# Keys transposed one phase at a time, one filter tile evacuated by VectorE, mixing outputs laid out anew, and new constants in the scheduler, in a gated mixer kernel

## The chip, the cores and the metric

The kernel runs on one core of one Trainium2 chip. The metric is the device time of one execution in microseconds (us), the median of several runs of the same kernel. The profile's span of an execution is 1.7 to 2.1 us shorter than its timed run, because it leaves out the start and the end of the execution.

Five engines matter. TensorE does the matmuls. VectorE does elementwise work and statistics. ScalarE mainly copies matmul results out of PSUM, the memory into which TensorE writes. GpSimd does small elementwise steps. SyncE issues the transfers (DMA). Each engine runs its own list of instructions in order, and engines wait for one another by semaphores. In the profile they are called PE (with PEld for weight loads), DVE, ACT, POOL and SP.

## The reference

The inputs are bfloat16, with S = 2048 positions and D = 640 channels. Two branches are computed from x and mixed by a gate.

```python
g = sigmoid((x * gate_w).sum(-1, keepdims=True))
# branch a: short filter of the keys, times v, long causal convolution by FFT, times q (q is x)
k_shift = sum over t < 4 of k_pad[:, t:t+S, :] * shift_k[:, 3-t]
kv = k_shift * v
y  = irfft(rfft(kv, 2S) * rfft(ssm_k, 2S))[:S] + kv * ssm_D
a  = q * y
# branch b: layernorm, then an MLP over the positions
h = layernorm(x)
u = gelu(einsum("bsd,sf->bdf", h, w1) + b1)
b = transpose(einsum("bdf,fs->bds", u, w2) + b2)
out = g * a + (1 - g) * b
```

## The kernel before

The convolution is a discrete Fourier transform done by matmuls with a table (`FTB` forward, `GTB` inverse). The positions are split into four phases (position modulo 4). TensorE transforms each phase, ScalarE copies the result to a slot of a tile `C`, and VectorE combines the slots with additions and subtractions of 128x2560 or 128x5120 elements. This is called mixing. The filter goes through it first. Then come the two halves of the product k_shift * v. The first is called `vkv` in the traces and the second `kv`. The matmuls that form k_shift have `KT`, the transposed keys, as the stationary operand and `DG`, a table of diagonal matrices, as the moving one. `X` is the layernormed input of the MLP, `ring` holds its weights, and `pp` is any PSUM buffer. In the layernorm, VectorE writes `stats` and `mv` (mean and variance), and GpSimd makes `rstd` (the reciprocal of the standard deviation) from `mv` in two short steps, `vtmp` and `rstd`. `junk` is the product with the gate's weights.

The keys are loaded with a transposing DMA in blocks of channels. The positions of one phase therefore lie four apart in a row, and the stationary operand is read with a stride of four elements:

```python
KT = [alloc(f"KT{i}", [128, ND, 1040], BF16) for i in range(2)]
def kT_load(h, db):
    dma(KT[h][:, db, 16:1040], A_k[0, 1024*h:1024*h+1024, db*128:db*128+128], ..., transpose=True, chain=True)
# in kv(hk): seven matmuls for each block of 128 channels
for q in range(4):
    items.append((..., V(KT[h], base + q, [[4, 128]]), DG[:, db, 0:4 - q, :]..., q == 0, False))
```

The filter is transposed on TensorE, and all 16 results (`wT`, 128x640) are copied by ScalarE:

```python
mms(vt, items, name="wtr")
act(wT[:, hk, p, :], full, ACT.Copy, vt=vt, name="wT")
```

The layernorm statistics of one 128x640 tile are four VectorE instructions. Two `bn_stats` each take half of the row, one `bn_aggr` reads what both wrote, and one product with the gate's weights needs neither.

```python
def ln_tile(hk, p):
    for ci in range(2):
        SC.add("DVE", 0.46, ... bn_stats(stats[..6*ci..], xs[.. 320*ci ..]) ...)
    SC.add("DVE", 0.2, ... bn_aggr(mv[:, t, :], stats[:, t, :]) ...)
    stt("DVE", junk[1][:, :], xs, 1.0, gwb[:, :], ALU.mult, ALU.mult, acc=gpre[:, t:t + 1])
```

The program does not fix the order of an engine's instructions. A list scheduler, run while the kernel is built, simulates all engines with an estimated duration for every operation and emits them in the order that its simulation starts them. When an operation ends, its successors become available after a latency:

```python
op.end = t + op.dur
free[e] = op.end
# ...
for s in op.succ:
    lat = 0.08 if s.eng == e else 0.15
    if e == "PE" and s.eng == "PE":
        lat = 0.0
    avail[s] = max(avail[s], op.end + lat)
```

The 0.08 applies to a successor on the same engine.

## Time and profile before

The time was 203.19 us (median of 4 runs, 203.11 to 203.23).

| Before | | Read from |
|---|---|---|
| span | 201.0 us | head of the page |
| TensorE busy | 187.1 us, 93% | busy time by engine |
| VectorE busy | 183.4 us, 91% | busy time by engine |
| TensorE without a gap | 73.91 to 197.91 us | chain of waits |
| second kv product, ready | 73.9 us | chain of waits |
| TensorE waiting for the kv product | 1.4 us | waits |

From the page of the kernel before, here are the span and the busy times:

```profile
span 201.0 us, 3282 instructions
...
PE 187.1 (93%) x1383; PEld 136.2 (68%) x1383; DVE 183.4 (91%) x204; ACT 102.9 (51%) x145; POOL 24.8 (12%) x24
...
PEclk9999999999999999999999999999999999999999
```

Two engines are above 90%, so busy shares don't tell which of them sets the time. The chain of waits does. Its columns are start in us, length in us, engine, what is written, source line and count.

```profile
22.12 0.75 DVE stats L825 x2
22.87 0.73 DVE junk L629 x2
23.61 0.13 DVE mv L827
...
23.82 2.70 POOL vtmp L621
...
26.59 1.05 POOL rstd L611
...
72.37 1.50 DVE kv L611
...
73.91 124.00 PE pp L293 x910
```

VectorE and its short exchanges with GpSimd hold the chain nearly alone from about 10 us until it has written the last kv product. After that the chain is one unbroken piece of TensorE work, 910 matmuls of 136 ns each, and 3.1 us remain after it. So the time is the end of the last kv product, plus the TensorE work that isn't done by then, plus a tail.

The key matmuls and their weight loads are in the timeline of TensorE, and in the groups by shape (group, then busy time in us and mean ns of one, then idle time before them):

```profile
61.89 7.13 PE L293 MATMUL pp<-DG,KT 128*128 128x512 bf16 x56
68.86 3.42 PE L293 MATMUL pp<-X,ring 128*128 128x320 bf16 x24
```

```profile
L293 PEld LDWEIGHTS pp<-DG,KT 128*128 128x128 bf16 x140 | 13.1, 115 | 5.5 <-DMA KT<-in_A_k_dram 1.2 <-issue 0.5
```

From one start to the next, these 56 matmuls take 6.97 us, or 0.871 us for the seven of a block. The weight loads take 115 ns each, beside the matmuls.

### The profile page before, as it was taken

The numbers are of one execution on the slowest core, as the hardware profiler recorded it, in microseconds if no ns is written. First come the engines' busy times: TensorE is split into PE (matmuls) and PEld (weight loads), VectorE is DVE, ScalarE is ACT, GpSimd is POOL, SyncE is SP. The second block draws the span as 40 slices with busy tenths as digits, with TensorE's granted clock in tenths as the row PEclk, the third lists the DMA queues.
The fourth block names the chain that finished last, engine by engine and source line by source line (L and its number), as shares of the span: only waits on it lengthen the run. The fifth ranks groups of instructions, "written<-read, shape, count | busy, mean of one in ns | idle before, by whom it ended". The sixth has DMA issues, their size and how long they took to land.

```text
span 201.0 us, 3282 instructions
## 1 busy us (share of the span) xinstructions
PE 187.1 (93%) x1383; PEld 136.2 (68%) x1383; DVE 183.4 (91%) x204; ACT 102.9 (51%) x145; POOL 24.8 (12%) x24
## 2 busy tenths in 40 slices
PE   0769989999999979999999999999999999999993
PEld 0456656576656747777777777788888887688672
DVE  7799979998997999999999999999999982899672
ACT  4798899965698658841111221131313136631762
POOL 1002245403033060000000005003100000000000
PEclk9999999999999999999999999999999999999999
DMA  5999999999940000007501805995999900311033
GB/s 158 344 406 348 284 160 201 305 344 231 221 176 0 0 3 0 0 3 234 183 0 34 273 10 103 160 360 218 166 273 341 359 14 0 130 68 65 0 138 126
DMA packets 35226, 32.37 MB, mean 161 GB/s; under 512 B 15618, under 2 KB 32652, under 8 KB 35212
## 3 DMA queue, kind: packets, MB, share of 16 engines
q1 hardware_dynamic: 34080, 29.53, 49.2%
q0 software_dynamic: 1088, 2.62, 8.1%
q8 instruction: 11, 0.18, 0.4%
q14 instruction: 3, 0.02, 0.0%
q10 hardware_dynamic: 44, 0.01, 0.0%
HBM read 23.25 MB, written 2.62 MB: 129 GB/s over the span
## 4 chain that ended last, share of the span: by engine, by line
PE 62%; DVE 25%; POOL 5%; DMA 4%; issue 2%; SPq 1%; ACT 0%
PE pp L293 62%; DVE stats L825 5%; DVE junk L629 5%; DVE C L611 5%; DMA gwb<-in_gate_w_dram 4%; POOL vtmp L621 3%; DVE X L622 3%; DVE SS L611 3%; POOL rstd L611 2%; DVE kv L611 1%; DVE vkv L611 1%; DVE mv L827 1%; SPq L267 1%; ACT O L649 0%; DVE O L611 0%
## 5 line engine op out<-in xcount | busy, mean ns | idle before, releaser
L293 PE MATMUL pp<-X,ring 128*128 128x320 bf16 x384 | 53.6, 299 | 0.0
L293 PE MATMUL pp<-GT,W 128*128 128x320 bf16 x384 | 52.8, 299 | 0.0
L293 PEld LDWEIGHTS pp<-GT,W 128*128 128x128 bf16 x384 | 43.4, 113 | 8.9 <-issue 0.2
L611 DVE TENSOR_TENSOR C<-C 128x2560 bf16<-128x2560 bf16 (+1 forms) x28 | 49.0, 1769 | 0.3
L293 PEld LDWEIGHTS pp<-X,ring 128*128 128x128 bf16 x384 | 37.5, 98 | 14.5
L649 ACT ACTIVATE C<-pp 128x640 bf16<-128x640 f32 x64 | 39.3, 752 | 7.1 <-PE pp L293 7.0
L649 ACT ACTIVATE O<-pp,c,omg 128x640 bf16<-128x640 f32 (+1 forms) x17 | 14.5, 853 | 36.7 <-PE pp L293 36.7
L649 ACT ACTIVATE GT<-pp,cc 128x640 bf16<-128x640 f32 x12 | 9.5, 793 | 33.7 <-PE pp L293 33.7
L611 DVE TENSOR_TENSOR tm<-C,C 128x5120 bf16<-128x5120 bf16 x8 | 22.2, 2817 | 0.0
L293 PE MATMUL pp<-wT,FTB 128*128 128x320 bf16 x128 | 19.8, 314 | 0.0
L293 PE MATMUL pp<-DG,KT 128*128 128x256 bf16 (+3 forms) x140 | 18.1, 288 | 0.6 <-DMA KT<-in_A_k_dram 0.6
L611 DVE TENSOR_TENSOR C<-tm 128x2560 bf16<-128x2560 bf16 x12 | 17.4, 1484 | 0.1
L293 PEld LDWEIGHTS pp<-DG,KT 128*128 128x128 bf16 x140 | 13.1, 115 | 5.5 <-DMA KT<-in_A_k_dram 1.2
L293 PEld LDWEIGHTS pp<-wT,FTB 128*128 128x128 bf16 x128 | 11.8, 102 | 7.4 <-ACT C L649 2.5
L649 ACT ACTIVATE cgb<-pp,gg 128x640 bf16<-128x640 f32 x16 | 12.7, 793 | 5.7 <-PE pp L293 5.7
L293 PE MATMUL pp<-ident,ssm 128*128 128x128 bf16 x80 | 8.8, 266 | 6.9 <-DMA ssm<-in_A_ssm_k_dram 5.6
L825 DVE BATCH_NORM_STATS2 stats<-X 128x6 f32<-128x320 bf16 x32 | 13.7, 464 | 1.2 <-DMA X<-in_A_q_dram 1.2
L649 ACT ACTIVATE ksh<-pp 128x1024 bf16<-128x1024 f32 (+1 forms) x12 | 10.1, 879 | 8.2 <-PE pp L293 8.2
L293 PE MATMUL pp<-C,GTB 128*128 128x320 bf16 x96 | 13.6, 299 | 0.0
L629 DVE SCALAR_TENSOR_TENSOR junk<-X,gwb 128x640 bf16<-128x640 bf16 x16 | 12.9, 803 | 0.2 <-DMA gwb<-in_gate_w_dram 0.2
L262 POOL DMA_DIRECT2D C<-C x4 | 5.1, 1506 | 61.1 <-DVE C L611 61.1
L293 PEld LDWEIGHTS pp<-ident,ssm 128*128 128x128 bf16 x80 | 6.3, 128 | 9.2 <-DMA ssm<-in_A_ssm_k_dram 5.6
(49 smaller groups left out, 163.1 us busy)
## 6 DMA issues: line engine op xcount, KB each, us to landing
ring<-in_B_w_dram SPq DMA_DIRECT2D x12, 512.0 KB, 8.5
W<-in_B_w_dram SPq DMA_DIRECT2D x8, 768.0 KB, 7.8
ssm<-in_A_ssm_k_dram SPq DMA_DIRECT2D x4, 640.0 KB, 9.0
X<-in_A_q_dram SPq DMA_DIRECT2D x4, 640.0 KB, 9.2
C<-C POOLq DMA_DIRECT2D x4, 640.0 KB, 9.1
out_dram<-O SPq DMA_DIRECT2D x7, 320.0 KB, 2.4
vkv<-in_A_v_dram SPq DMA_DIRECT2D x2, 640.0 KB, 5.0
v<-in_A_v_dram SPq DMA_DIRECT2D x2, 640.0 KB, 6.3
```

Of the source, the lines that this page charges most:

```text
L262: ins = engobj.dma_start(out_ap, in_ap, accum_op=ALU.add, max_dma_last_dim=2560)
L267: ins = engobj.dma_start(out_ap, in_ap)
L293: ins = self.nc.tensor.matmul(ps_ap, lhsT=lhsT, rhs=rhs, start=start, stop=stop, skip_group_check=True)
L611: return SC.add(eng, d, lambda s: T.op(eng, lambda e: e.tensor_tensor(o, a, b, op), [a, b], [o]), [a, b], [o], prio=prio, name="tt")
L621: return e.tensor_scalar(o, a, s1, None, op0=op0)
L622: return e.tensor_scalar(o, a, s1, s2, op0=op0, op1=op1)
L629: eng, lambda e: e.scalar_tensor_tensor(out=o, in0=a, scalar=sc, in1=b, op0=op0, op1=op1, accum_out=acc),
L649: return T.op("ACT", lambda e: e.activation(o, src, func, **kw), rr + [src], ww)
L825: SC.add("DVE", 0.46, (lambda o, i: lambda s: T.op("DVE", lambda e: e.bn_stats(o, i), [i], [o]))(o, i), [i], [o])
L827: SC.add("DVE", 0.2, (lambda o, i: lambda s: T.op("DVE", lambda e: e.bn_aggr(o, i), [i], [o]))(o, i), [i], [o])
```

## The change

The intent was this. If the keys are loaded one phase at a time, the stationary operand is contiguous and its weight load gets shorter. If VectorE takes one of the early filter tiles, ScalarE's queue gets shorter, and the first transform starts earlier. With the mixing outputs in other slots, operations can start when a part of their inputs is there. The scheduler's constants changed in the same diff. It is cut here to its core:

```diff
+    TAIL = {"PE": 0.15, "ACT": 0.13, "DVE": 0.08, "POOL": 0.1}
...
-                    op.end = t + op.dur
-                    free[e] = op.end
+                    free[e] = t + op.dur
+                    op.end = free[e] + self.TAIL[e]
...
-                    lat = 0.08 if s.eng == e else 0.15
-                    if e == "PE" and s.eng == "PE":
-                        lat = 0.0
-                    avail[s] = max(avail[s], op.end + lat)
+                    a_ = op.end + 0.1
+                    if s.eng == e and e in self.TAIL and op.lat >= 0:
+                        a_ = free[e]
+                    avail[s] = max(avail[s], a_)
...
+WTD = {(0,2,1)}
-        KT = [alloc(f"KT{i}", [128, ND, 1040], BF16) for i in range(2)]
+        KT = [alloc(f"KT{i}", [128, ND, 4, 272], BF16) for i in range(2)]
...  (fixed parts of the estimates of VectorE and ScalarE operations about halved, matmuls a little longer)
-        def kT_load(h, db):
-            dma(KT[h][:, db, 16:1040], A_k[0, 1024 * h:1024 * h + 1024, db * 128:db * 128 + 128], ..., transpose=True, chain=True)
+        def kT_load(h, p):
+            dma(KT[h][:, :, p, 16:272], dr(A_k, (1024 * h + p) * D, [[4 * D, 256], [1, D]]), ..., transpose=True, chain=True)
...
-            act(wT[:, hk, p, :], full, ACT.Copy, vt=vt, name="wT")
+            if (h, p, kt) in WTD:
+                evac_dve(wT[:, hk, p, :], full, vt)
+            else:
+                act(wT[:, hk, p, :], full, ACT.Copy, vt=vt, name="wT")
...  (mixing)
-                tt("DVE", sl(Th, Ts + i, n), sl(R, i, n), sl(R, 2 + i, n), ALU.add)
-                tt("DVE", sl(R, i, n), sl(R, i, n), sl(R, 2 + i, n), ALU.subtract)
+                tt("DVE", sl(Th, Ts + i), sl(R, i), sl(R, 2 + i), ALU.subtract)
+                tt("DVE", sl(R, 2 + i), sl(R, i), sl(R, 2 + i), ALU.add)
...  (the remaining four outputs of mixing are exchanged between R and Th in the same way)
-                                      V(KT[h], base + q, [[4, 128]]), DG[:, db, 0:4 - q, :]...
+                                      V(KT[h], base + 272 * q, [[1, 128]]), DG[:, db, 0:4 - q, :]...
```

More of the change, by code (lines that the diff above doesn't have):

```diff
@@ L396, in run @@
         free = {e: 0.0 for e in engs}
-        dma_free = 0.0
+        dma_free = 1.4
         avail = {}
@@ L464, in run @@
                     if op.vt.left == 0:
-                        heapq.heappush(frees, (op.end + 0.05, op.vt.slot, op.vt.cls))
+                        heapq.heappush(frees, (op.end + 0.1, op.vt.slot, op.vt.cls))
                 for s in op.asucc:
@@ L505 @@
 STATS_ACT = ()
+MIXW, MIXA0, MIXA1, V1DMA = "", "", "", False
+WTD = {(0,2,1)}
 def _build(nc, A_q, A_k, A_v, A_shift_k, A_ssm_k, A_ssm_D, B_x, B_w1, B_b1, B_w2, B_b2, gate_w, out):
@@ L591, in _build @@
         tm = [alloc(f"tm{i}", [128, 2, 4, D], BF16, at=E_base + 2 * SL * 2 * i) for i in range(2)]
-        q_lo = alloc("q_lo", [128, 2, 4, D], BF16, at=base_of(C[1]) + 2 * SL * 2)
-        q_hi = alloc("q_hi", [128, 2, 4, D], BF16, at=base_of(C[0]))
+        q_lo = alloc("q_lo", [128, 2, 4, D], BF16, at=base_of(C[1]))
+        q_hi = alloc("q_hi", [128, 2, 4, D], BF16, at=base_of(C[0]) + 2 * SL * 2)
         cgb = [alloc(f"cgb{i}", [128, 2, D], BF16, at=base_of(FTB) + 2560 * i) for i in range(3)]
@@ L602, in dve_dur @@
         def dve_dur(n, mode):
-            return n / {1: 960.0, 2: 1920.0, 4: 3840.0}[mode] + (0.1 if mode == 4 else 0.16)
+            return n / {1: 960.0, 2: 1920.0, 4: 3840.0}[mode] + (0.04 if mode == 4 else 0.08)
         def act_dur(n, nap=0):
-            return n / 1200.0 + 0.19 + 0.09 * nap
+            return n / 1200.0 + 0.085 + 0.04 * nap
         def tt(eng, o, a, b, op, mode=2, prio=None):
@@ L661, in mms @@
         def mms(vt, items, prio=None, name="mm"):
-            dur = sum(max(n_of(r) / 2400.0, 0.117) for _, _, r, _, _ in items)
+            dur = sum(max(n_of(r) / 2400.0 * 1.008, 0.12) for _, _, r, _, _ in items)
             rd = []
@@ L709, in w1_load @@
             dma(ring[c % 2][:, 4 * hk:4 * hk + 4, :], dr(B_w1, 512 * hk * F + 512 * c, [[4 * F, 128], [F, 4], [1, 512]]), 128 * 4096, chain=True)
-        def kT_load(h, db):
-            dma(KT[h][:, db, 16:1040], A_k[0, 1024 * h:1024 * h + 1024, db * 128:db * 128 + 128], 128 * 2048, rate=170.0, transpose=True, chain=True)
+        def kT_load(h, p):
+            dma(KT[h][:, :, p, 16:272], dr(A_k, (1024 * h + p) * D, [[4 * D, 256], [1, D]]), 256 * D * 2, rate=170.0, transpose=True, chain=True)
         def v_load(hk):
@@ L738, in _build @@
             w1_load(0, hk)
-        for db in range(ND):
-            kT_load(0, db)
+        for p in range(4):
+            kT_load(0, p)
         T_PI = float(np.float32(math.pi * (1.0 - 1e-6)))
@@ L798, in fwd, with acc_dma, hv, mixing @@
                     act(o, two, ACT.Copy, vt=vt, name=name + "e", **kw)
-        def mixing(R, Th, Ts, fine=False):
+        def acc_dma(dst, src, n):
+            return dma(dst, src, 128 * n * 4, stream="POOL", prio=0, accum=True)
+        def hv(hs, i):
+            h, s = hs
+            return V(h, (s + i) * SL, [[1280, 2], [1, 1280]])
+        def mixing(R, Th, Ts, how):
             def sl(h, s, n=1):
@@ L805, in pr @@
                 return V(h, s * SL + (1280 if rev else 0), [[-1280 if rev else 1280, 2], [1, 1280]])
-            for i, n in (((0, 1), (1, 1)) if fine else ((0, 2),)):
-                tt("DVE", sl(Th, Ts + i, n), sl(R, i, n), sl(R, 2 + i, n), ALU.add)
-                tt("DVE", sl(R, i, n), sl(R, i, n), sl(R, 2 + i, n), ALU.subtract)
-            tt("DVE", sl(R, 2), sl(Th, Ts), sl(Th, Ts + 1), ALU.add)
-            tt("DVE", sl(R, 3), sl(Th, Ts), sl(Th, Ts + 1), ALU.subtract)
-            oA = V(Th, (Ts + 1) * SL, [[-1280, 2], [1, 1280]])
-            oB = V(Th, Ts * SL, [[3 * 1280, 2], [1, 1280]])
-            tt("DVE", oA, pr(R, 0), pr(R, 1, True), ALU.add)
-            tt("DVE", oB, pr(R, 0), pr(R, 1, True), ALU.subtract)
+            for i in range(2):
+                tt("DVE", sl(Th, Ts + i), sl(R, i), sl(R, 2 + i), ALU.subtract)
+                if how == "dma":
+                    acc_dma(hv((R, 2), i), hv((R, 0), i), SL)
+                else:
+                    tt("DVE", sl(R, 2 + i), sl(R, i), sl(R, 2 + i), ALU.add)
+            oA = V(R, 1 * SL, [[-1280, 2], [1, 1280]])
+            oB = V(R, 0, [[3 * 1280, 2], [1, 1280]])
+            tt("DVE", oA, pr(Th, Ts), pr(Th, Ts + 1, True), ALU.add)
+            tt("DVE", oB, pr(Th, Ts), pr(Th, Ts + 1, True), ALU.subtract)
+            tt("DVE", sl(Th, Ts), sl(R, 2), sl(R, 3), ALU.add)
+            tt("DVE", sl(Th, Ts + 1), sl(R, 2), sl(R, 3), ALU.subtract)
         def ln_tile(hk, p):
@@ L824, in ln_tile @@
                     o, i = stats[:, t, 6 * ci:6 * ci + 6], xs[:, 320 * ci:320 * ci + 320]
-                    SC.add("DVE", 0.46, (lambda o, i: lambda s: T.op("DVE", lambda e: e.bn_stats(o, i), [i], [o]))(o, i), [i], [o])
+                    SC.add("DVE", 0.41, (lambda o, i: lambda s: T.op("DVE", lambda e: e.bn_stats(o, i), [i], [o]))(o, i), [i], [o])
                 o, i = mv[:, t, :], stats[:, t, :]
-                SC.add("DVE", 0.2, (lambda o, i: lambda s: T.op("DVE", lambda e: e.bn_aggr(o, i), [i], [o]))(o, i), [i], [o])
+                SC.add("DVE", 0.13, (lambda o, i: lambda s: T.op("DVE", lambda e: e.bn_aggr(o, i), [i], [o]))(o, i), [i], [o])
             stt("DVE", junk[1][:, :], xs, 1.0, gwb[:, :], ALU.mult, ALU.mult, acc=gpre[:, t:t + 1])
@@ L855, in _build @@
                 tt("DVE", DG[:, :, :, :], V(ident, 0, [[0, 5], [0, 4], [1, 128]]), shkf, ALU.mult, mode=1)
-                mixing(C[0], SS, 0, fine=True)
+                mixing(C[0], SS, 0, MIXW)
             else:
-                mixing(C[1], C[0], 0)
+                mixing(C[1], C[0], 2, MIXW)
         gate_op = act(gth[:, :], gpre[:, :], ACT.Tanh, scale=0.5)
@@ L863, in _build @@
         tt("POOL", c2[:, :].rearrange("p (a b) -> p a b", a=4), omg[:, :].rearrange("p (a b) -> p a b", a=4), b2f, ALU.mult)
-        memset("POOL", KT[0][:, :, 12:16], 0.0)
+        memset("POOL", KT[0][:, :, :, 15:16], 0.0)
         for hk in range(2):
@@ L869, in _build @@
             w1_load(1, hk)
-        for db in range(ND):
-            kT_load(1, db)
+        for p in range(4):
+            kT_load(1, p)
         for hk in range(2, 4):
@@ L877, in ap @@
                 return V(h, s * SL + o, [[SL, 2], [st, 2], [1, D]])
-            tt("DVE", ap(Vh, Vs, 0, 3 * D), ap(Vh, Vs, 0, 3 * D), ap(Wh, Ws, 2 * D, -D), ALU.add)
             tt("DVE", ap(Vh, Vs, D, D), ap(Vh, Vs, D, D), ap(Wh, Ws, 3 * D, -3 * D), ALU.subtract)
-        v1mix(C[0], 2, C[1], 2)
-        v1mix(SS, 0, C[0], 0)
+            if V1DMA:
+                for i in range(2):
+                    acc_dma(V(Vh, (Vs + i) * SL, [[3 * D, 2], [1, D]]), V(Wh, (Ws + i) * SL + 2 * D, [[-D, 2], [1, D]]), 2 * D)
+            else:
+                tt("DVE", ap(Vh, Vs, 0, 3 * D), ap(Vh, Vs, 0, 3 * D), ap(Wh, Ws, 2 * D, -D), ALU.add)
+        v1mix(SS, 0, C[0], 2)
+        v1mix(C[0], 0, C[1], 0)
         def kv(hk):
@@ L892, in kv @@
                     db = d0 + b
-                    base = db * 1040 + 16 + 512 * kt
+                    base = db * 1088 + 16 + 128 * kt
                     for q in range(4):
                         items.append(((lambda s, b=b, q=q: s[:, 512 * b + 128 * q:512 * b + 512]),
-                                      V(KT[h], base + q, [[4, 128]]), DG[:, db, 0:4 - q, :].rearrange("p a b -> p (a b)"), q == 0, False))
+                                      V(KT[h], base + 272 * q, [[1, 128]]), DG[:, db, 0:4 - q, :].rearrange("p a b -> p (a b)"), q == 0, False))
                     for q in range(1, 4):
                         items.append(((lambda s, b=b, q=q: s[:, 512 * b:512 * b + 128 * q]),
-                                      V(KT[h], base - 4 + q, [[4, 128]]), DG[:, db, 4 - q:4, :].rearrange("p a b -> p (a b)"), False, q == 3))
+                                      V(KT[h], base - 1 + 272 * q, [[1, 128]]), DG[:, db, 4 - q:4, :].rearrange("p a b -> p (a b)"), False, q == 3))
                 mms(vt, items, name="kv")
@@ L910, in _build @@
             kv(hk)
-        SC.add("POOL", 0.3, lambda s: T.op("POOL", lambda e: e.tensor_copy(KT[1][:, :, 12:16], KT[0][:, :, 1036:1040]), [KT[0][:, :, 1036:1040]], [KT[1][:, :, 12:16]]),
-               [KT[0][:, :, 1036:1040]], [KT[1][:, :, 12:16]])
+        SC.add("POOL", 0.3, lambda s: T.op("POOL", lambda e: e.tensor_copy(KT[1][:, :, :, 15:16], KT[0][:, :, :, 271:272]), [KT[0][:, :, :, 271:272]], [KT[1][:, :, :, 15:16]]),
+               [KT[0][:, :, :, 271:272]], [KT[1][:, :, :, 15:16]])
         for p in PORD:
             fwd(lambda kt, p, ci: vkv0[:, kt, p, 320 * ci:320 * ci + 320], 0, p, C[2], p, None, "A")
-        mixing(C[2], C[1], 0)
+        mixing(C[2], C[1], 2, MIXA0)
         for hk in range(2, 4):
@@ L919, in _build @@
             fwd(lambda kt, p, ci: kv1[:, kt, p, 320 * ci:320 * ci + 320], 1, p, C[3], p, None, "A")
-        mixing(C[3], C[2], 0)
+        mixing(C[3], C[2], 2, MIXA1)
         for ft in range(FT):
@@ L967, in _build @@
                     act(O1[:, hk, p, :].rearrange("p (a b) -> p a b", a=2), two, ACT.Identity, bias=c2[:, t:t + 1], scale=omg[:, t:t + 1], vt=vt, name="o1")
-        A0 = {0: (C[2], 2), 1: (C[1], 0)}
-        A1 = {0: (C[3], 2), 1: (C[2], 0)}
-        V0 = {0: (C[0], 2), 1: (SS, 0)}
-        V1 = {0: (C[1], 2), 1: (C[0], 0)}
+        A0 = {0: (C[1], 2), 1: (C[2], 0)}
+        A1 = {0: (C[2], 2), 1: (C[3], 0)}
+        V0 = {0: (SS, 0), 1: (C[0], 0)}
+        V1 = {0: (C[0], 2), 1: (C[1], 0)}
         def P2(hs, rev=False):
@@ L990, in product @@
             tt("DVE", H(dst, 1), H(T1, 0), H(T1, 1), ALU.add)
-        C3a = (C[3], 0)
-        def acc_dma(dst, src):
-            (hd, sd), (hs, ss) = dst, src
-            for i in range(2):
-                o = V(hd, (sd + i) * SL, [[1280, 2], [1, 1280]])
-                i_ = V(hs, (ss + i) * SL, [[1280, 2], [1, 1280]])
-                dma(o, i_, 128 * 5120 * 2, stream="POOL", prio=0, accum=True)
+        C3a = (C[3], 2)
         def y1(g):
@@ L1003, in y1 @@
             product(V1[g], A0[g], V1[g])
-            acc_dma(A1[g], V1[g])
+            for i in range(2):
+                acc_dma(hv(A1[g], i), hv(V1[g], i), SL)
         def invmix(Ya, Yb, sc, z0, z2):
```

## The prediction

> **What bounds the kernel.** In the chain of waits TensorE holds 62% of the 201.0 us span, as one unbroken piece from 73.9 to 197.9 us (910 matmuls, 136 ns each); before it stands VectorE, nearly alone, from about 9 us to the product kv at 73.86 us, which releases that piece. So the time is: when VectorE finishes the last kv product, plus the TensorE work not yet done by then, plus a 3 us tail. TensorE's losses before 73.9 us sum to about 13 us (timeline): 5.5 in the filter transposes to 13.8 us, 1.6 and 2.1 where ScalarE evacuates a 128x640 tile every 0.60 us, 0.5 waiting for transposed keys at 49 us, 1.4 for kv at 72.5 us.
>
> **Contiguous stationary keys: nothing.** The second key stretch streams 56 matmuls (8 blocks of 2048 columns) in 6.97 us (61.89 to 68.86), 0.871 us a block. The Trainium skill ("TensorE: Matmul & The Clock Gate", section "Wait — 56ns, not 53.3ns?") gives N/2.4 + 2.5 ns a matmul, which is 0.871 us for these seven. So it streams at its floor although the operand has a stride of four. Weight loads are 115 ns each against 98 for contiguous ones, but hidden; I expect the record to fall to about 98 and the stretch to stay at 0.87 us a block. The transposing loads (12.7 us of issue for one half of the keys) I expect about as long; the second half is needed some 15 us later in the new order, so the 0.5 us wait goes.
>
> **One filter tile on VectorE.** ScalarE loses one of its 0.65 us evacuations and is better ordered: the first filter transform should start near 12.6 instead of 13.9 us. But VectorE gets about 0.8 us, on the chain.
>
> **Mixing.** Same element count (1.4 us per 128x2560 operation, 2.8 per 128x5120), six more instructions, nearly no time.
>
> **Order moved.** From the built order: 104 instead of 48 of the 320-column MLP matmuls stand before the last kv product. That is 56 x 136 ns = 7.6 us of work pulled forward, some into the 0.60 us evacuation gaps. But VectorE has 13 instead of 7 mixing-sized units before that product, 6 x 1.41 = 8.5 us, plus 0.8 for the tile, less about 1 because a GpSimd rstd step no longer sits behind a 2.8 us VectorE operation. I estimate the last kv product at about 82.3 us and TensorE solid from there for 854 matmuls of 136 ns: to 198.8 us, against 197.9. Also, TensorE should run out of work before vkv is ready: keys end near 47.5, 16 MLP matmuls near 49.7, vkv ready at about 52.7 us: a new wait near 3 us, which swallows the early gain. In the late stage VectorE should stay 3 to 4 us ahead of the inverse transforms, and the tail is unchanged.
>
> **Prediction.** 203.5 us (203.19 before), a shift of +0.9 on the sum, pulled slightly down because the reordering may hide more than I count; 201.4 to 205.7 should hold it 8 times in 10. Faster by over 2%: 0.05; within 2%: 0.89; slower by over 2%: 0.06.
>
> **What would show it.** Key stretch 0.87 us a block; weight loads of it near 98 ns; TensorE waiting about 3 us for the vkv product near 50 us; last kv product near 82 us, and about 116 us of unbroken TensorE after it; VectorE busy 183 to 185 us.
>
> **What would make it wrong.** VectorE reaching the products earlier or later than my sum; slower transposing loads (keys needed near 38 us); TensorE's clock dropping after the new wait; a new wait of the inverse transforms on VectorE after 156 us, where they now stand 9 us earlier.

## The result

The changed kernel took 209.15 us (median of 4 runs, 209.1 to 209.76; the profiled run is the one of 209.76) and its results are correct. It is slower by 3.0%: the ratio is 1.0301, with a 95% interval of 1.0281 to 1.032. Every ratio here is the mean time of the fast runs of one kernel over that of the kernel before in the same rounds, so it is not quite the ratio of the medians quoted.

The page of the changed kernel, the same three lines as above:

```profile
span 207.8 us, 3275 instructions
...
PE 190.3 (92%) x1379; PEld 136.9 (66%) x1383; DVE 188.2 (91%) x211; ACT 103.4 (50%) x144; POOL 21.2 (10%) x24
...
PEclk9999999999769999999999999999999999999999
```

VectorE is busy 4.8 us longer, where I had expected up to 1.6. TensorE's granted clock dips in two slices. The chain of waits of the changed kernel:

```profile
22.79 0.81 DVE stats L842 x2
23.60 0.02 issue
23.62 0.21 DVE mv L844
23.83 0.70 DVE junk L632 x2
...
26.43 3.48 POOL rstd L614
...
53.91 1.41 DVE vkv L614
...
145.67 11.85 DMA C<-C
...
157.62 1.50 DVE C L614
...
159.14 2.91 DVE C L614 x2
...
162.19 42.55 PE pp L293 x312
```

The last unbroken piece of TensorE starts only at 162.19 us, released by VectorE. VectorE in turn had waited for the accumulating transfer `C<-C`, 11.85 us long. The span is 162.19 + 42.55 + a tail of 3.1 = 207.8 us. The waits of TensorE show two entries that were not there before (us in total, times, longest):

```profile
PE pp L293 <- DVE vkv L614: 4.1, 1, 4.1
...
PE pp L293 <- DVE C L614: 1.1, 1, 1.1
```

After the 4.1 us wait the matmuls are slow for a while, as the timeline of TensorE shows:

```profile
55.37 1.78 PE L293 MATMUL pp<-vkv,FTB 128*128 128x320 bf16 x6 [4.11 <-DVE vkv L614]
56.94 2.34 PE L293 MATMUL pp<-X,ring 128*128 128x320 bf16 x8
59.08 2.30 PE L293 MATMUL pp<-vkv,FTB 128*128 128x320 bf16 x8
61.21 1.26 PE L293 MATMUL pp<-X,ring 128*128 128x320 bf16 x8
```

These 22 matmuls took 5.84 us (55.37 to 61.21), 265 ns each instead of 136. The Trainium skill ("TensorE: Matmul & The Clock Gate", section "What's actually happening") says that TensorE drops to half its clock after about 3.4 us of idling. This trace roughly agrees: the granted clock was 0.50 from 54.39 us, 3.1 us into the wait, to 61.21. One run below does not: in a_ln a wait of 2.04 us was followed by a granted clock of 0.50 from 52.92 to 56.33 us, so the page's figure is not a safe limit.

The last kv product ended at 84.77 + 1.49 = 86.26 us, by the timeline of VectorE:

```profile
84.77 1.49 DVE L614 TENSOR_TENSOR kv<-ksh,v 128x2560 bf16<-128x2560 bf16 x1
```

The prediction had 82.3 us. This is where to dig: why did VectorE get there 4 us later than a sum of its instructions said?

The answer is visible in one layernorm tile. First the timeline of VectorE before, one tile from its statistics to the next tile's:

```profile
41.96 0.83 DVE L825 BATCH_NORM_STATS2 stats<-X 128x6 f32<-128x320 bf16 x2
42.71 0.81 DVE L629 SCALAR_TENSOR_TENSOR junk<-X,gwb 128x640 bf16<-128x640 bf16 x1
43.44 0.08 DVE L629 DVE_READ_ACCUMULATOR junk<-X,gwb 128x1 f32 x1
43.44 0.20 DVE L827 BATCH_NORM_AGGREGATE mv<-stats 128x2 f32<-128x12 f32 x1
43.56 0.83 DVE L825 BATCH_NORM_STATS2 stats<-X 128x6 f32<-128x320 bf16 x2
```

And the changed kernel:

```profile
43.08 0.88 DVE L842 BATCH_NORM_STATS2 stats<-X 128x6 f32<-128x320 bf16 x2
44.00 0.21 DVE L844 BATCH_NORM_AGGREGATE mv<-stats 128x2 f32<-128x12 f32 x1
44.12 0.77 DVE L632 SCALAR_TENSOR_TENSOR junk<-X,gwb 128x640 bf16<-128x640 bf16 x1
44.82 0.08 DVE L632 DVE_READ_ACCUMULATOR junk<-X,gwb 128x1 f32 x1
44.82 0.88 DVE L842 BATCH_NORM_STATS2 stats<-X 128x6 f32<-128x320 bf16 x2
```

These are the same four operations. Before, the gate product stands between the statistics and the aggregate that reads them, and each instruction starts about 0.08 us before the one ahead of it ends: the tile takes 43.56 - 41.96 = 1.60 us. In the changed kernel the aggregate comes right behind the statistics. It starts 0.04 us after they end, and the tile takes 44.82 - 43.08 = 1.74 us. In both built programs the aggregate waits on VectorE's own semaphore; what differs is whether the operation that it waits for stands directly ahead. I counted in the built order: of the 16 aggregates ahead of the last kv product, 16 stand right behind their statistics in the changed kernel and none did before. That is 16 x 0.14 = 2.2 us. The mixing operations that depend on the one directly ahead show it too, also where they only overwrite what that one reads. Here the second waits for the first and the third waits for neither, so the starts lie 1.52 and then 1.41 us apart:

```profile
31.37 1.49 DVE L614 TENSOR_TENSOR SS<-C 128x2560 bf16<-128x2560 bf16 x1
32.89 1.49 DVE L614 TENSOR_TENSOR C<-C 128x2560 bf16<-128x2560 bf16 x1
34.30 1.49 DVE L614 TENSOR_TENSOR SS<-C 128x2560 bf16<-128x2560 bf16 x1
```

The first mixing's eight operations take 11.7 us (31.45 to 43.17), against 11.2 before (29.17 to 40.78, less a statistics instruction of 0.41 that stands among them).

### The profile page after: what moved, and what is told of

It is laid out like the page before. It is cut to its first block, busy times and chain, and to the rows that moved or that the text cites. A ratio compares the mean times of both kernels' runs of the same rounds, so it can differ in the third digit from the quotient of the medians.

```text
span 207.8 us, 3275 instructions
## 1 busy us (share of the span) xinstructions
PE 190.3 (92%) x1379; PEld 136.9 (66%) x1383; DVE 188.2 (91%) x211; ACT 103.4 (50%) x144; POOL 21.2 (10%) x24
## 4 chain that ended last, share of the span: by engine, by line
DVE 40%; PE 40%; DMA 8%; ACT 4%; POOL 4%; issue 1%; DVEq 0%
PE pp L293 40%; DVE C L614 15%; DVE tm L614 11%; DMA C<-C 6%; DVE stats L842 4%; DVE junk L632 3%; DVE SS L614 3%; POOL rstd L614 3%; DMA ssm<-in_A_ssm_k_dram 2%; ACT C L652 2%; DVE X L625 2%; DVE vkv L614 1%; DVE mv L844 1%; POOL vtmp L624 1%; ACT wT L652 1%
## 5 line engine op out<-in xcount | busy, mean ns | idle before, releaser
L293 PE MATMUL pp<-X,ring 128*128 128x320 bf16 x384 | 55.9, 303 | 0.0
L614 DVE TENSOR_TENSOR C<-C 128x2560 bf16<-128x2560 bf16 x34 | 49.7, 1489 | 4.7 <-ACT C L652 2.6
L652 ACT ACTIVATE C<-pp 128x640 bf16<-128x640 f32 x64 | 40.7, 734 | 18.2 <-PE pp L293 18.2
L293 PE MATMUL pp<-wT,FTB 128*128 128x320 bf16 x128 | 20.9, 321 | 0.1
L293 PE MATMUL pp<-DG,KT 128*128 128x384 bf16 (+3 forms) x136 | 17.2, 285 | 0.3 <-issue 0.2
L293 PE MATMUL pp<-vkv,FTB 128*128 128x320 bf16 x64 | 12.2, 337 | 5.1 <-DVE vkv L614 4.1
L293 PEld LDWEIGHTS pp<-DG,KT 128*128 128x128 bf16 x140 | 11.9, 98 | 5.6 <-issue 0.3
L842 DVE BATCH_NORM_STATS2 stats<-X 128x6 f32<-128x320 bf16 x32 | 14.4, 483 | 0.3 <-DMA X<-in_A_q_dram 0.3
L293 PEld LDWEIGHTS pp<-vkv,FTB 128*128 128x128 bf16 x64 | 6.2, 107 | 10.2 <-DVE vkv L614 4.4
L293 PEld LDWEIGHTS pp<-C,GTB 128*128 128x128 bf16 x96 | 9.3, 98 | 5.0 <-issue 1.4
```

The costliest lines, as they stand in the source:

```text
L293: ins = self.nc.tensor.matmul(ps_ap, lhsT=lhsT, rhs=rhs, start=start, stop=stop, skip_group_check=True)
L614: return SC.add(eng, d, lambda s: T.op(eng, lambda e: e.tensor_tensor(o, a, b, op), [a, b], [o]), [a, b], [o], prio=prio, name="tt")
L652: return T.op("ACT", lambda e: e.activation(o, src, func, **kw), rr + [src], ww)
L842: SC.add("DVE", 0.41, (lambda o, i: lambda s: T.op("DVE", lambda e: e.bn_stats(o, i), [i], [o]))(o, i), [i], [o])
```

## The experiments

The theories were these.

- **Order theory.** The new scheduler model drops the latency between dependent operations of one engine, so it packs them back to back. On the chip that costs VectorE, whose chain sets the time.
- **Clock theory.** The 4.1 us wait halves TensorE's clock, and the matmuls lost there are the time lost.
- **Parts theory.** One of the three named parts (keys, tile, mixing) costs the time by itself. (Mixing was never run alone; its worth follows only from differences.)

Twelve kernels ran, in four groups, each against runs of the kernel before on the same chip. Its median was 202.96 to 203.01 us in all four groups. All kernels give correct results.

### 1. Keep TensorE busy in the wait (a_fill)

Dummy matmuls stand ahead of the wait, in a group whose first real matmul overwrites what they wrote, so the result is unchanged.

```diff
+NFILL = 28
...
+                    extra = []
+                    if name == "A" and h == 0 and p == 0 and k2 == 0 and c == 0:
+                        extra = [(chk(i % 2), FTB[:, 0, 0, 0, 0, :], X[:, 0, 0, 0:320], True, True) for i in range(NFILL)]
+                    mms(vt, extra + items, name=name, skip=len(extra))
```

> The changed kernel with 28 needless 320-column matmuls put into the TensorE wait for the second vkv product (their result is overwritten; every engine's order is otherwise unchanged). Clock theory: the 4.1 us wait lets TensorE's clock fall to half, and the 22 matmuls after it take 5.8 us in place of 3.0; with the array kept busy they run at 136 ns, the vkv product is ready at the same 55.3 us, and the kernel gets about 2.5 us faster, to 206.6 us. Rival, that only VectorE's lateness counts and the slow matmuls would be hidden later: 208.8 us or more.

The median was 209.15 us, ratio 1.0301 (1.0284 to 1.0318), so nothing was gained. The edit did what it should: the granted clock was 1.0, and the wait shrank from 4.11 to 0.30 us. The timeline of TensorE of this run shows where the time went:

```profile
55.38 0.99 PE L293 MATMUL pp<-vkv,FTB 128*128 128x320 bf16 x6 [0.30 <-DVE vkv L615]
...
86.30 1.53 PE L293 MATMUL pp<-kv,FTB 128*128 128x320 bf16 x10 [1.50 <-DVE kv L615]
```

TensorE, now faster, waits 1.50 us for the kv product, which comes at the same 86.3 us, and later 1.62 us for the inverse (1.15 in the changed kernel). The clock theory fell: the clock loss was real, 2.85 us of it (22 matmuls at 265 instead of 136 ns), but in the median run it was hidden under VectorE's chain. The profiled run of the changed kernel is the slowest of its four, 0.6 us above the median, and its mean granted clock was 0.984 against 0.990 to 0.992 in the others; there TensorE was still 0.7 us late when the last kv product came (matmuls on it start at 86.98 us).

### 2. Move the aggregate behind the gate product (a_ln)

```diff
-                SC.add("DVE", 0.13, ... bn_aggr ...)
             stt("DVE", junk[1][:, :], xs, 1.0, gwb[:, :], ALU.mult, ALU.mult, acc=gpre[:, t:t + 1])
+            SC.add("DVE", 0.13, ... bn_aggr ...)
```

> The changed kernel with the layernorm aggregate issued after the gate product in place of directly after the two statistics it reads. Dependency theory: an instruction that reads what the one just before it on VectorE wrote costs about 0.14 us more, so a tile takes 1.60 in place of 1.74 us, the second vkv product is ready near 53.5 in place of 55.3 us, TensorE's wait falls to about 2.4 us, and the kernel gets 1.7 us faster, or 4.5 if the clock then holds (204.6 to 207.4 us). Rival, that the filter tile on VectorE and the longer list of operations before the product made it late: a tile still 1.74 us, 209 us.

The median was 207.13 us (206.79 to 207.76; the profiled run is the slowest), ratio 1.0206 (1.0184 to 1.0228), so 2.0 us came back. The tile takes 1.60 us again (43.03 to 44.63 from one aggregate to the next). The last kv product ended at 83.0 instead of 86.26 us: 2.2 of these 3.26 us are the tiles, and 1.0 is less waiting for `rstd` (2.5 in place of 3.5 us). So the aggregate's place explains most of the lateness of the product, but only 2.0 us of it reached the end. The chain of waits shows what stopped the rest:

```profile
81.59 1.41 DVE kv L614
...
83.05 73.80 PE pp L293 x542
156.85 2.35 issue
159.20 43.64 PE pp L293 x320
```

TensorE stops for 2.35 us ahead of the inverse. The profile puts it down to "issue", but VectorE had waited 2.91 us for the accumulating transfer `C<-C` (to 154.68 us), and the third of the mixing operations behind that wait ended at 159.10 us, just before TensorE went on. That VectorE released it is inferred from these times; experiment 8 tests it.

### 3. Put the same-engine latency back (a_dep)

This is the changed kernel with one condition edited. Successors on the same engine, other than on TensorE, get a latency again.

```diff
-                    if s.eng == e and e in self.TAIL and op.lat >= 0:
+                    if s.eng == e and e == "PE":
                         a_ = free[e]
```

> The changed kernel with one line of its scheduler's model put back: a successor on the same engine other than TensorE sees its input later than the end of the instruction before it, so that the scheduler puts something else in between. Dependency theory: mixing operations before the vkv product take 1.40 in place of 1.49 us and layernorm tiles 1.60 us; second vkv product ready near 53 us, TensorE's wait 2 us or less, clock full: 203 to 205 us. Rival, that the new order of the work as such (more MLP matmuls early, more mixing before the last products) is what costs: 207 us or more.

The median was 203.71 us, ratio 1.0037 (1.0021 to 1.0054): 5.4 of the 6.0 us are back. No aggregate stands right behind its statistics any more. The chain of waits:

```profile
81.08 1.41 DVE kv L614
...
82.54 116.19 PE pp L293 x854
```

This is the prediction's picture: a last kv product near 82.3 us, then 854 matmuls in 116 us. The first mixing is back at 11.2 us (29.86 to 41.86, less two statistics instructions of 0.40). The order theory stands, with its size.

### 4. The keys alone (e1_keys)

This is the kernel before with the new layout and loads of the keys (the `KT`, `kT_load` and `kv` lines of the diff), and nothing else.

> The kernel before with only the keys changed: transposed one phase at a time, contiguous stationary operands. My theory: key matmuls still at 0.87 us for a block of 2048 columns, weight loads 98 in place of 115 ns and still hidden; the time moves only through the scheduler's new order, 202.5 to 204.5 us. Rival, that strided stationary operands slow TensorE: blocks clearly under 0.87 us and 1 us or more gained.

The median was 203.05 us, ratio 1.0001 (0.9986 to 1.0016). The weight loads are shorter, as the group by shape shows, and the matmuls still take 0.87 us a block:

```profile
L293 PEld LDWEIGHTS pp<-DG,KT 128*128 128x128 bf16 x140 | 11.9, 98 | 6.1 <-ACT C L649 0.6 <-issue 0.3
```

Contiguous keys are worth nothing here, and cost nothing. The scheduler's order moved with them (the last kv product ended at 78.07 in place of 73.85 us), so the time is that of the keys and this order together; the 0.87 us a block is the keys' own.

### 5. The scheduler model alone (e2_sched)

This is the kernel before with only the time model of the changed kernel: all the scheduler lines of the diff and the changed estimates. The operations are those of before; only their order and timing differ.

> The kernel before with nothing changed but the time constants and latencies of the scheduler's model (those of the change); the work, its layout and its buffers are those of before. Dependency theory: the order alone makes the kernel slow, layernorm tiles take 1.74 in place of 1.60 us, the last kv product comes late, 206 to 209 us. Rival, that the filter tile on VectorE, the new mixing layout or the keys make it slow: 203 to 204 us.

The median was 207.51 us, ratio 1.0223 (1.0207 to 1.0238). Of the 16 aggregates, 15 stand right behind their statistics. The chain of waits:

```profile
84.72 1.41 DVE kv L612
...
86.19 116.19 PE pp L293 x854
```

So 4.5 us of slowdown (207.51 against 202.96 us in the same group) come with none of the three named parts. GpSimd's part in it is the `rstd` step. It takes 1.05 us when it runs alone and 3.48 us in this run, twice, where it meets a long VectorE operation (`DG` and a 128x5120 mixing operation). In the changed kernel it meets the 2.82 us operation that builds `DG` (26.18 to 29.00 us) and takes 3.48 us, as its chain of waits above shows. The Trainium skill ("SBUF — State Buffer", section "SBUF: two separate sides") says that VectorE and GpSimd share a pair of memory ports, that a VectorE operation with two inputs in SBUF locks it against a GpSimd operation that reads SBUF, and that the one that comes second is fully blocked. The stretching agrees with that: the step ends 0.91 us after the `DG` operation does. Before, the stretched step was the one ahead of it, `vtmp`, at 2.70 us beside the same operation, so the stretching is not new; it moved to the longer of the two steps.

### 6. Everything but the scheduler model (a_oldsched)

The mirror image is the changed kernel with keys, tile and mixing, and the time model of before.

```diff
-    TAIL = {"PE": 0.15, "ACT": 0.13, "DVE": 0.08, "POOL": 0.1}
...
-                    a_ = op.end + 0.1
-                    if s.eng == e and e in self.TAIL and op.lat >= 0:
-                        a_ = free[e]
-                    avail[s] = max(avail[s], a_)
+                    lat = 0.08 if s.eng == e else 0.15
+                    if e == "PE" and s.eng == "PE":
+                        lat = 0.0
+                    avail[s] = max(avail[s], op.end + lat)
...  (and the old estimates)
```

> The changed kernel with all three stated parts (keys, tile on VectorE, new mixing layout), and the scheduler's whole time model put back as it was before: the mirror image of the run that put the new model alone into the kernel before (207.5 us). If the order that the model makes is the whole cause of the slowdown, the three parts together cost nothing: 201.8 to 203.7 us (the keys gave 203.05, keys and tile 202.3), with the layernorm tile at 1.60 us again. If the new mixing layout costs VectorE something of its own, 204 us or more.

The median was 202.51 us, ratio 0.9975 (0.9958 to 0.9991). The three named parts together, without the new model, are 0.5 us faster than before (203.00 in their group). TensorE doesn't wait for a product any more, and its chain of waits ends in one piece:

```profile
67.45 128.52 PE pp L293 x948
```

The four corners side by side (each group's own runs of the kernel before were at 202.96 to 203.19 us):

| | old time model | new time model |
|---|---|---|
| kernel before | 203.19 us, 0 of 16 aggregates right behind | 207.51 us (e2_sched), 15 of 16 |
| all three parts | 202.51 us (a_oldsched), 0 of 16 | 209.15 us, 16 of 16 |

The parts theory fell: no part costs the time by itself. But the corners do not simply add. Under the old model the parts gain 0.5 us, and under the new one they cost 1.6 (ratio 1.0301 against 1.0223). The order changes with the parts in both; what makes the difference was not isolated. Of the new model's lines, one condition is worth 5.4 us (a_dep), and the others together about 1.2 (203.71 against 202.51).

### 7. The tile on VectorE, alone and in other orders (e1_tile, a_dep_notile)

In e1_tile the kernel before has the new keys and the one tile on VectorE:

```diff
+            if (h, p, kt) == (0, 2, 1):
+                evac_dve(wT[:, hk, p, :], full, vt)
+            else:
                 act(wT[:, hk, p, :], full, ACT.Copy, vt=vt, name="wT")
```

> The kernel before with the keys one phase at a time and the one filter tile on VectorE, old mixing, old order model; to be held against the run with the keys alone (203.05 us, ratio 1.0001). If VectorE's chain sets the time as in the changed kernel, the tile adds its 0.83 us: 203.9 us. If the start of the filter transform is what counts, it falls by up to 1.3 us: 201.8 us. Expected: 203.2 to 204.2 us.

It took 202.29 us, ratio 0.9962 (0.9946 to 0.9979). I had expected a small loss. With the keys alone the ratio was 1.0001, so the tile gains about 0.8 us here. The first filter transform starts at 13.28 instead of 13.90 us, and TensorE doesn't wait for the last kv product.

In a_dep_notile the one-condition repair of experiment 3 has all tiles on ScalarE (`WTD = set()`).

> The changed kernel with the same-engine latency put back in the model (as in the run before) and the filter tile back on ScalarE. If VectorE's chain up to the last kv product sets the time, its 0.83 us come off it whole: last kv product near 81.7 us, 202.9 us. Rival, that TensorE's earlier start was worth more than VectorE's time: 204.3 us or more.

It took 204.47 us, ratio 1.0074 (1.0059 to 1.0089), against 1.0037 with the tile: slower, and I had expected it faster. VectorE reached the last kv product only 0.34 us earlier, and the scheduler put 8 matmuls fewer ahead of it (862 remain in place of 854, 1.17 us). The whole order shifts with one tile, so this pair doesn't isolate the tile's own value.

### 8. More matmuls ahead of the inverse (a_ln_acc)

This is experiment 2 with the scheduler told that accumulating transfers land 4 us later, so that 40 second-layer matmuls go ahead of the inverse.

```diff
-                    op.end = dma_free + 2.0
+                    op.end = dma_free + (2.0 if op.lat >= -1.0 else -op.lat)
...  (accumulating transfers get lat=-6.0)
```

> The kernel with the layernorm aggregate after the gate product, and in the scheduler's model 4 us more for the accumulating copies, so that 40 MLP matmuls stand before the inverse transforms. Theory: the 2.35 us that TensorE lost there at 157 us, waiting for VectorE, which waited for such a copy, were whole on the critical path: 204.8 us. Rival, that the wait only moves: 206.5 us or more.

The median was 205.19 us, ratio 1.0109 (1.0093 to 1.0126), 1.9 us faster than a_ln. TensorE runs through from 83.00 us with 862 matmuls. The wait ahead of the inverse was on the critical path.

### 9. Looking for a faster version (a_tune, a_tune_tile, b_tune)

In a_tune the version of experiment 3 without the tile, with the later landing of experiment 8, gets durations from the trace in its model: matmuls of n/2400 + 0.0027 us without a lower bound, the GpSimd steps at 1.05 and 0.8 us, and the statistics at 0.38 us.

> An attempt at a better version: the changed kernel with the same-engine latency put back, the filter tile on ScalarE, the accumulating copies 4 us longer in the model, and the model's durations of small matmuls and of GpSimd set to the measured ones. If the theory is right that VectorE's time to the last kv product plus the rest of TensorE's work is the time: last kv product near 80.5 us with no wait after it, 202 to 203 us. If the reordering brings a new wait: 203.5 us or more.

The median was 201.4 us, ratio 0.9922 (0.9908 to 0.9937), the fastest kernel and 0.8% faster than the kernel before. That is below the 202 to 203 us I had expected: the last kv product ended at 78.5 us and not at 80.5. TensorE waits for VectorE only 0.3 us in all. Its chain of waits ends in one piece:

```profile
72.89 123.41 PE pp L293 x909
```

Then the tile went back to VectorE (`WTD = {(0,2,1)}`).

> The fastest version so far (201.4 us; the changed kernel with a scheduler model that has measured durations and the same-engine latency, all filter tiles on ScalarE) with one edit: the early filter tile goes back to VectorE. If the tile's 0.83 us on VectorE lies wholly on the chain that sets the last kv product, the time is 202.2 us. If the earlier start of the first filter transform (1.3 us on TensorE and ScalarE) pays for it here, where TensorE no longer waits for the kv product, 200.5 to 201.4 us. The scheduler reorders what follows, so a difference below 0.5 us is not the tile's alone.

It took 202.47 us, ratio 0.9973 (0.9959 to 0.9988), so here the tile costs 1.1 us. Its copy waits 1.08 us for TensorE and starts at 12.32 us, where in e1_tile it started at 9.72. The first filter transform starts at 13.21 us, no earlier than without the tile (13.01). A tile moved in order to start a transform early pays only where the transform does start early. That is argued from two orders, not isolated.

Last, b_tune is the kernel before with the keys and the measured durations in its own model, with the old mixing layout.

```diff
-            dur = sum(max(n_of(r) / 2400.0, 0.117) for _, _, r, _, _ in items)
+            dur = sum(n_of(r) / 2400.0 + 0.0027 for _, _, r, _, _ in items)
...  (and the GpSimd and ScalarE estimates)
```

> The kernel before, its old mixing layout and its own order model with its latencies, but with the keys one phase at a time and with the measured durations of matmuls and GpSimd operations in the model. If the new mixing layout is what made the 201.4 us version possible, this stays near 203 us (202.5 to 203.5). If the durations in the model are what matters and the layout does nothing, 200.5 to 202 us.

It took 207.86 us, ratio 1.0238 (1.0222 to 1.0253), outside both expectations. TensorE never waits for VectorE here. The first filter transform starts at 16.02 us (13.90 before), and TensorE waits 4.6 us for ScalarE's copies of the filter tiles (2.4 before). Durations close to the measured ones did not make a good order by themselves. Its tail after the last matmul is also longer, 4.8 in place of 3.1 us. Whether a_tune needs the new mixing layout stays open, because b_tune lost most of its time at these two places.

## Why the prediction was wrong

The prediction said 203.5 us (201.4 to 205.7), and it was 209.15 us.

- **How the time is made up: right.** Where TensorE has one unbroken piece at the end, its start, its length and a tail of 3.1 us give the span: 82.54 + 116.19 + 3.1 = 201.8 (a_dep), 86.19 + 116.19 + 3.1 = 205.5 (e2_sched), 72.89 + 123.41 + 3.1 = 199.4 (a_tune), and 162.19 + 42.55 + 3.1 = 207.8 for the changed kernel.
- **"I estimate the last kv product at about 82.3 us": the step that failed.** It came at 86.26 us. I took the durations of VectorE's instructions from the trace of before and counted units in the new order (73.86 + 6 x 1.41 + 0.8 - 1 = 82.1, which I rounded up). Those durations belong to before's neighbours. The layernorm tile isn't a constant 1.60 us. It is 1.74 us when the aggregate follows its statistics directly. Summed from start to start in the two traces, the 16 tiles take 28.1 us in place of 26.1. The 21 mixing operations ahead of the product take 30.6 us, where 1.41 us each would be 29.6.
- **"less about 1 because a GpSimd rstd step no longer sits behind a 2.8 us VectorE operation": wrong.** In the new order the step starts beside that operation and takes 3.48 us. VectorE's waits for `rstd` sum to 3.5 us against 3.3 before, so the 1 us I took off was not there and 0.2 was added. With 2.0 and 1.0, these terms add up to 4.2 us, where 86.26 lies 4.1 above the sum. That addition is arithmetic on two traces, but two runs bear it out: moving the aggregates takes 3.26 us off the last kv product, the `rstd` wait included (83.0 in a_ln), and putting the whole condition back takes off another 0.5 (82.49 in a_dep).
- **"VectorE should stay 3 to 4 us ahead of the inverse transforms": wrong.** TensorE waited 1.15 us for VectorE at 162 us. The late accumulating transfer (VectorE waited 1.65 us for it) belongs to the same place. The late product is not the whole reason: in a_ln it came at 83.0 us, and the stop there was longer, 2.35 us. The order counts too: 200 second-layer matmuls stand ahead of the inverse in the changed kernel and 192 in a_ln, but 232 in a_ln_acc and 256 in a_dep, which have no such stop. In the profiled run these terms account for the miss: I had TensorE end its unbroken piece at 198.8 us, and it ended at 162.19 + 42.55 = 204.74. Of these 5.9 us, 3.95 are the product, 0.7 pass until TensorE, still late from its slow matmuls, takes it up at 86.98 us, and 1.15 are this wait. (The 0.7 belong to the profiled run, which is 0.6 us above the median.)
- **"A new wait near 3 us" for vkv: right in kind, too small.** It was 4.1 us, because the product came at 55.3 and not at 52.7 us. The drop of the clock that I had listed as a risk came with it. Without it TensorE would have been ready in time, but only to wait for VectorE instead (a_fill, same median).
- **Contiguous keys worth nothing: right.** In the changed kernel, as in e1_keys, loads of 98 ns stand where they were 115, and a block takes 0.87 us. The Trainium skill ("TensorE: Matmul & The Clock Gate", section "Wait — 56ns, not 53.3ns?") gives N/2.4 + 2.5 ns a matmul, and the traces agree: 0.871 us for a block's seven, and 136 ns at 320 columns.
- **Tile and mixing: nearly nothing, right in size under the old model.** All three parts together gave -0.5 us there (a_oldsched), and 1.6 us more time under the new one. The first filter transform started at 12.62 us, as predicted (12.6).
- **What I passed over.** I read the scheduler lines of the diff only through the built order, as counts of matmuls and units, and did not look at which instruction stands directly behind which. The built order showed the aggregate behind its statistics, on a wait for its own engine.

## What to carry to other kernels

An instruction that waits for the one directly ahead of it on the same engine loses the overlap that independent neighbours have; here that was about 0.11 to 0.14 us each on VectorE, so a scheduler's model must keep a same-engine latency, and an estimate for a new order must look at pairs of neighbours, not only at counts. When a stall or a clock drop is visible on one engine, fill it before blaming it: if the time stays, another engine's chain sets it. When a diff changes both operations and the model that orders them, run the four corners, since here the named parts were worth -0.5 us under the old model and +1.6 under the new, and the unnamed model +4.5 to +6.6.

## What the Trainium skill lacked or had wrong

- "VectorE: DVE Perf Modes", section "The DRAIN you can't avoid", says that a semaphore wait between VectorE operations costs nothing extra, on the measure of eight copies. Here it does. The same four layernorm instructions take 1.74 us where the aggregate waits for the statistics directly ahead of it and 1.60 us where an independent instruction stands between, and 128x2560 mixing operations lie 1.52 us apart from start to start where the second depends on the first, and 1.41 where it does not.
- The same section has the next operation start after the pipe is empty, and points to another section for operations that are not held and start earlier, without saying by how much. In these traces independent neighbours start about 0.08 us before the recorded end of the one ahead (42.71 against 42.79 us in the kernel before), and only the waiting one starts after it (44.00 against 43.96 in the changed kernel).
- "TensorE: Matmul & The Clock Gate", section "LDWEIGHTS (loading the stationary operand)", gives P/1.2 with P the columns, 107 ns for 128 of them. The records show 98 ns for a contiguous operand and 115 for one with a stride of four, both hidden. No difference between the two is stated there.
- "SBUF — State Buffer", section "SBUF: two separate sides", states the lock between VectorE and GpSimd without the duration of a blocked operation. Here a GpSimd step of 1.05 us is recorded as 3.48 us beside a 2.82 us VectorE operation.
